# An attention block with its gradients on one core: a product moved to per-head pieces, a re-ordered iteration, reserved VectorE slots, and V transposed as float32 pairs

## Chip, cores, metric

The kernel runs on one core of a Trainium2 chip. The metric is the device time of one execution in microseconds, median of several runs. "Granted clock" is the share of the full TensorE (PE) clock that the throttle let through.

## The reference

A decode step (two batches, one query each) of an attention block and a ReLU MLP, with all gradients (shortened):

```python
def _A_ref(x, k_cache, v_cache, wq, wo):      # x: 2x1x640, caches: 2x32x4096x128, bf16
    q = (x @ wq).reshape(B, Sq, Hq, Dh).transpose(0, 2, 1, 3)
    scores = jnp.einsum("bhqd,bhkd->bhqk", q, k_cache) * (Dh ** -0.5)
    p = _softmax(scores, axis=-1)
    o = jnp.einsum("bhqk,bhkd->bhqd", p, v_cache)
    return o.transpose(0, 2, 1, 3).reshape(B, Sq, Hq * Dh) @ wo
h  = x + _A_ref(_layernorm(x), k_cache, v_cache, wq, wo)
h2 = h + relu(_layernorm(h) @ w1) @ w2
# outputs: h2 and the gradients of x, both caches, wq, wo, w1 and w2
```

Each cache holds 64 MiB and both have gradients as large. V is read twice, so the kernel moves 372.7 MB.

## The kernel before

Pass 1 is a software pipeline over 64 (batch, head) pairs: iteration `i` transposes K of pair `i` on PE and multiplies it by q, makes the softmax of pair `i-1`, and finishes the value product of pair `i-2`. `yield` marks the places where background work (`bg`) may be put in. The code issues the instructions in this order; the timeline of the changed kernel below shows VectorE at its own in that order (226.65 to 227.89 us).

```python
def p1_iter(i, dve_group):
    # step 0: c["KT0"] = transpose_group(c["K"], 0)       PE transposes, ScalarE copies to SBUF
    # step 1: u_half(0), KT1, max over partitions (PE) and gmax (VectorE), m_part(0)
    # step 2: scores group 0, KT2, exp (ScalarE), u_half(1), m_part(1)
    # step 3: scores group 1, KT3, m_part(2), pk_part(0)  pk = K times softmax, VectorE
    # step 4: scores group 2, m_part(3), pk_part(1)
    # step 5: m_part(4), m_part(5), sum and its reciprocal, P_bf, pk_part(2)   (VectorE)
    # step 6: scores group 3, rmax, m_part(6), pk_part(3)
    ...
    # step 7
        m_part(7)
        nc.scalar.activation(out=MT[:], in_=r["m"][:, 0:128], func=ACT.Copy, scale=r["rtot"][:, 0:1])
        nc.scalar.activation(out=OU[:, br, hr, :], in_=r["m"][:, 128:130], ...)   # attention output of a head
```

After the last head of a batch a background generator does that batch's middle, beginning with the product with `wo`:

```python
def middle_gen(b):
    nc.vector.tensor_copy(out=OFc[:, :, b], in_=OU[:, b, :, 0])
    yield
    a_ps = pst([128, ND], FP32, "mid", "a_ps")
    for c in range(ND):
        for h in range(H):
            nc.tensor.matmul(a_ps[:, c:c + 1], lhsT=wo_t[:, h, c * 128:(c + 1) * 128], rhs=OFc[:, h, b:b + 1],
                             start=(h == 0), stop=(h == H - 1))
            if h % (4 if b == 0 else 8) == 3:
                yield
    ...  # norm, MLP, its gradients, reductions on VectorE (ttr), gradient of the attention output
```

Pass 2 reads V again (`W`), transposes it for the product with that gradient, and writes two outer products per pair, the gradients of V and of K. It starts 15 iterations after the last head of batch 0; until pass 1 ends, every second iteration carries one step of it ("the mix").

## Time and profile before

| | before |
|---|---|
| time, median | 1045.99 us |
| DMA busy (16 engines' mean) | 954 of 1044 us, 391 GB/s while busy |
| PE / VectorE / ScalarE busy | 81% / 67% / 62% |
| mean granted clock | 0.74 |

The prediction below shows the stages, chain and waits. One line is added here. It is the share of each engine in the chain of work that ended last, followed back from the last instruction, from the page:

```profile
PE 40%; DMA 26%; DVE 16%; issue 10%; ACT 5%; POOL 1%; SPq 0%; POOLq 0%; ACTq 0%; DVEq 0%
```

And these are two cost groups of the page: line, engine, operation, output<-inputs, shapes, count, busy us and mean ns, idle time before it and what ended it. They are the transposes of V and ScalarE's copies of all transposes.

```profile
L279 ACT COPY t_sb<-t_ps 128x1024 bf16<-128x1024 bf16 x489 | 490.4, 1013 | 190.4 <-PE t_ps L274 184.1
L274 PE MATMUL t_ps<-ident_bf,Wt 128*128 128x128 bf16 x2048 | 239.2, 289 | 16.6 <-DMA Wt<-in_A_v_cache_dram 15.3
```

A transpose of V kept PE busy for 239.2/2048 = 117 ns.

### The profile page before, as it was taken

How to read it: one execution, taken by the hardware profiler on the slowest of the kernel's cores; microseconds unless marked ns; L12 is line 12 of the kernel's file. 1: busy time of each engine (PE TensorE's matmuls, PEld its weight loads, DVE VectorE, ACT ScalarE, POOL GpSimd, SP SyncE). 2: the span in 40 equal slices, each digit the busy share in tenths (PEclk: the TensorE clock that was granted, in tenths of full speed). 3: DMA queues.
4: the chain of work that ended last, by engine and by line, in shares of the span. 5: the costliest groups of instructions: out<-in, count | busy, mean ns of one | idle time of the engine just before them, and what ended most of it. 6: DMA issues, size and time to landing. Idle time of an engine off the chain costs nothing.

```text
span 1044.0 us, 32292 instructions
## 1 busy us (share of the span) xinstructions
PE 843.8 (81%) x14111; PEld 730.7 (70%) x14111; DVE 698.8 (67%) x1654; ACT 644.8 (62%) x985; POOL 95.2 (9%) x216
## 2 busy tenths in 40 slices
PE   6999989999998988878895665547998987676795
PEld 5988888889987887778784554436675765665553
DVE  3656777766549777776665768777876755566465
ACT  4555555467766586667674564546777766555684
POOL 0000000000000000000011111111111111111121
PEclk9988999899969889887875575566555555667555
DMA  9999999999857578898999999999899998999697
GB/s 350 382 400 405 363 364 379 347 349 351 323 206 282 205 278 314 346 379 342 363 413 425 371 384 394 355 402 361 326 412 422 398 393 329 421 422 401 231 374 319
DMA packets 59758, 372.70 MB, mean 357 GB/s; under 512 B 5760, under 2 KB 15424, under 8 KB 17376
## 3 DMA queue, kind: packets, MB, share of 16 engines
q1 hardware_dynamic: 38960, 221.50, 56.2%
q0 software_dynamic: 20656, 149.14, 34.7%
q8 instruction: 110, 1.80, 0.7%
q14 instruction: 32, 0.26, 0.1%
HBM read 221.48 MB, written 149.13 MB: 355 GB/s over the span
## 4 chain that ended last, share of the span: by engine, by line
PE 40%; DMA 26%; DVE 16%; issue 10%; ACT 5%; POOL 1%; SPq 0%; POOLq 0%; ACTq 0%; DVEq 0%
PE t_ps L274 16%; DMA out_dram<-gV 15%; PE m_ps L304 9%; DMA Wt<-in_A_v_cache_dram 6%; DVE pk L310 5%; DVE gK L550 4%; PE o_ps L652 4%; PE m_ps L320 4%; PE s_ps L285 3%; DVE junk L436 3%; ACT t_sb L279 2%; DMA Vt<-in_A_v_cache_dram 2%; DMA Kt<-in_A_k_cache_dram 2%; PE dp_ps L285 1%; DVE gV L550 1%
## 5 line engine op out<-in xcount | busy, mean ns | idle before, releaser
L279 ACT COPY t_sb<-t_ps 128x1024 bf16<-128x1024 bf16 x489 | 490.4, 1013 | 190.4 <-PE t_ps L274 184.1
L274 PE MATMUL t_ps<-ident_bf,Wt 128*128 128x128 bf16 x2048 | 239.2, 289 | 16.6 <-DMA Wt<-in_A_v_cache_dram 15.3
L274 PEld LDWEIGHTS <-Wt 128*128 128x128 bf16 x2048 | 185.4, 132 | 67.7 <-issue 50.0
L285 PEld LDWEIGHTS <-t_sb 128*128 128x128 bf16 x4096 | 171.1, 104 | 67.4 <-ACT t_sb L279 58.5
L310 DVE TENSOR_TENSOR pk<-Kt,ep 128x1024 bf16<-128x1024 bf16 x256 | 174.5, 683 | 45.0 <-ACT ep L353 41.2
L550 DVE TENSOR_TENSOR gV<-rb,pp 128x2048 bf16<-128x2048 bf16 x128 | 155.8, 1217 | 66.8 <-DMA out_dram<-gK 31.7
L550 DVE TENSOR_TENSOR gK<-rb,gsp 128x2048 bf16<-128x2048 bf16 x128 | 153.6, 1218 | 59.5 <-DMA out_dram<-gV 59.5
L304 PE MATMUL m_ps<-pk,Vt 128*128 128x129 bf16 x2048 | 193.3, 234 | 0.0
L274 PE MATMUL t_ps<-ident_bf,Kt 128*128 128x128 bf16 x2048 | 172.9, 234 | 2.3 <-DMA Kt<-in_A_k_cache_dram 2.3
L304 PEld LDWEIGHTS <-Vt 128*128 128x128 bf16 x2048 | 135.8, 104 | 4.5
L274 PEld LDWEIGHTS <-Kt 128*128 128x128 bf16 x2048 | 132.4, 104 | 3.6 <-DMA Kt<-in_A_k_cache_dram 2.7
L285 PE MATMUL dp_ps<-goc,t_sb 128*128 128x1 bf16 x2048 | 97.6, 169 | 45.7 <-ACT t_sb L279 43.4
L594 POOL DMA_DIRECT2D out_dram<-gV x64 | 34.2, 534 | 667.7 <-DVE gV L550 638.1
L285 PE MATMUL s_ps<-qc,t_sb 128*128 128x1 bf16 x2048 | 89.3, 164 | 4.2 <-DVE gsp L585 2.0
L406 ACT ACTIVATE MT<-m_ps,rtot 128x128 bf16<-128x128 f32 x64 | 23.5, 368 | 105.3 <-PE m_ps L304 105.3
L320 PEld LDWEIGHTS <-Kt 128*128 128x128 bf16 x2048 | 64.7, 97 | 20.3 <-issue 18.9
L277 DVE COPY t_sb<-t_ps 128x1024 bf16<-128x1024 bf16 x43 | 29.7, 690 | 71.6 <-PE t_ps L274 71.5
L320 PE MATMUL m_ps<-ep,Kt 128*128 128x1 bf16 x2048 | 70.8, 164 | 7.6 <-ACT OU L407 6.3
L655 ACT CAST ot<-o_ps 128x512 bf16<-128x512 f32 (+3 forms) x120 | 59.8, 526 | 11.7 <-PE o_ps L652 10.4
L564 ACT CAST rb<-rb_ps 128x256 bf16<-128x256 f32 x64 | 24.4, 381 | 49.7 <-DVE gK L550 37.9
L610 POOL DMA_DIRECT2D out_dram<-gK x64 | 34.0, 531 | 226.8 <-DVE gK L550 183.7
L436 DVE CUSTOM_DVE_ANT_0 junk<-wo_t,hbc 128x640 bf16<-128x640 bf16 x64 | 52.1, 815 | 0.1
(168 smaller groups left out, 703.2 us busy)
## 6 DMA issues: line engine op xcount, KB each, us to landing
Kt<-in_A_k_cache_dram SPq DMA_DIRECT2D x64, 1024.0 KB, 8.0
Vt<-in_A_v_cache_dram SPq DMA_DIRECT2D x64, 1024.0 KB, 7.6
Wt<-in_A_v_cache_dram SPq DMA_DIRECT2D x64, 1024.0 KB, 10.6
out_dram<-gV POOLq DMA_DIRECT2D x64, 1024.0 KB, 8.2
out_dram<-gK POOLq DMA_DIRECT2D x64, 1024.0 KB, 9.3
wo_t<-in_A_wo_dram SPq DMA_DIRECT2D x4, 1280.0 KB, 9.5
wqs<-in_A_wq_dram SPq DMA_DIRECT2D x5, 1024.0 KB, 17.4
out_dram<-ot POOLq DMA_DIRECT2D x5, 1024.0 KB, 5.5
```

The source lines that it names most:

```text
L274: nc.tensor.transpose(t_ps[:, j, :], nat[:, g * GT + j, :], ident_bf[:])
L279: nc.scalar.copy(out=t_sb[:], in_=t_ps[:])
L285: nc.tensor.matmul(dst[:, sc:sc + 1], lhsT=t_sb[:, j, :], rhs=vec, start=True, stop=True)
L304: nc.tensor.matmul(r["m"][:, 0:129], lhsT=r["V"][:, sc, :], rhs=r["pk"][sc // GT][:, sc % GT, 0:129], start=False, stop=(sc == NSC - 1))
L310: nc.vector.tensor_tensor(out=pk[:, :, 0:128].rearrange("p s (a two) -> p s a two", two=2), in0=p["K"][:, sl, :].rearrange("p s (a two) -> ...
L320: nc.tensor.matmul(r["m"][:, 129:130], lhsT=r["K"][:, sc, :], rhs=r["ep"][:, sc, 0:1], start=(sc == 0), stop=False)
L436: nc.vector.tensor_tensor_reduce(out=junk[0:kc, 0:width], in0=in0, in1=in1, scale=1.0, scalar=0.0, op0=ALU.mult, op1=ALU.add, accum_out=acc)
L550: nc.vector.tensor_tensor(out=pairs_view(dst[:, sl, :]), in0=row.rearrange("p (a two) -> p a two", two=2)[:, None, :, :].to_broadcast([128 ...
L594: nc.gpsimd.dma_start(out=natural(out_3, b, h), in_=gV[:])
L610: nc.gpsimd.dma_start(out=natural(out_2, bp, hp), in_=gK[:])
L652: nc.tensor.matmul(o_ps[0:P, 0:nn], lhsT=L[:, bass.ds(c0 + k, P, step=cc)], rhs=R[:, n0:n0 + nn], start=True, stop=True)
L655: nc.scalar.copy(out=ot[0:P, k, n0:n0 + nn], in_=o_ps[0:P, 0:nn])
```

## The change

Its intent: spread the wo product over pass 1 so that pass 2 starts after 12 iterations rather than 15; give PE work while the softmax chain goes over VectorE; put the 0.8 us reductions into chosen gaps; and halve ScalarE's copies of V by moving pairs of bf16 as one float32. The core of the diff, cut:

```diff
+    def a_head():                       # wo product per head
+        b, h = pairs[a_next[0]]
+        if h == 0:
+            a_bank[0] = pst([128, ND], FP32, "a", "a_ps")
+        nc.vector.tensor_copy(out=OFc[:, h, b:b + 1], in_=OU[:, b, h, 0:1])
+        for c in range(ND):
+            nc.tensor.matmul(a_bank[0][:, c:c + 1], lhsT=wo_t[:, h, c * 128:(c + 1) * 128], rhs=OFc[:, h, b:b + 1],
+                             start=(h == 0 and c == 0), stop=(h == H - 1 and c == ND - 1))
+        a_next[0] += 1
...
+            if k == 5:                  # after step 5 of the iteration
+                a_heads(i)              # up to two a_head()s, from iteration 15 on
...                                      # iteration re-ordered
             c["KT0"] = transpose_group(c["K"], 0)
+            c["KT1"] = transpose_group(c["K"], 1)
...
+    def turn():                         # VectorE slots: a reduction waits for its turn
+        while slot[0] <= 0:
+            yield 0.0
+        slot[0] -= 1
...                                      # V as float32 pairs
+        natf = nat[:].bitcast(FP32)
+        for j in range(GT // 2):
+            cc = (g * GT) // 2 + j
+            nc.tensor.transpose(t_ps[:, j, :], natf[:, 2 * cc:2 * cc + 2, :].rearrange("p c k -> p (c k)"), ident_f[:])
...
-    M0_ITERS = 15
+    M0_ITERS = 12
...                                      # V of pass 2 asked for one step ahead
+        ahead = plan[n + 1][1] if n + 1 < len(plan) and ii is not None else jj
```

The row of coefficients for the pairs (`gom`) is made by a small selection product, `pair_rows`. The order of pass 2 also changed (gradient of K first), the final outer products got a third PSUM bank, and small softmax results moved into the bank of the scores. Smaller edits are not shown: the weights load in another order, and the credit by which background work is put in has a cap.

More of the change, by code (lines that the diff above doesn't have):

```diff
@@ L54 @@
     GH = 8
-    NMT = 52
+    NMT = 48
     def f_kc(c):
@@ L69 @@
     ps = ctx.enter_context(tc.tile_pool(name="ps", bufs=1, space=bass.MemoryType.PSUM))
-    PSB = {"tps": 2, "sps": 3, "m": 1, "tiny": 1, "mid": 1}
+    PSB = {"tps": 2, "sps": 3, "m": 1, "a": 1, "mid": 1}
     def pst(shape, dtype, tag, name):
@@ L90 @@
                             fill=1.0, base=0, pattern=[[-1, 128]], channel_multiplier=1)
-    ones_bf = const.tile([128, 128], BF16)
-    nc.vector.memset(ones_bf[:], 1.0)
-    ones_f32 = const.tile([128, 128], FP32)
-    nc.vector.memset(ones_f32[:], 1.0)
+    ident_f = const.tile([128, 128], FP32)
+    nc.vector.tensor_copy(out=ident_f[:], in_=ident_bf[:])
+    sel = const.tile([128, 2, 2, 64], BF16)
+    nc.gpsimd.memset(sel[:], 0.0)
+    for par in range(2):
+        nc.gpsimd.affine_select(out=sel[:, par, :, :], in_=sel[:, par, :, :], compare_op=ALU.not_equal,
+                                fill=1.0, base=-par, pattern=[[0, 2], [-2, 64]], channel_multiplier=1)
+    ones_bfc = const.tile([128, 1], BF16)
+    nc.vector.memset(ones_bfc[:], 1.0)
+    ones_bf = ones_bfc[:].to_broadcast([128, 128])
+    ones_f32c = const.tile([128, 1], FP32)
+    nc.vector.memset(ones_f32c[:], 1.0)
+    ones_f32 = ones_f32c[:].to_broadcast([128, 128])
     xr = cols.tile([4 * ND, 128], BF16)
@@ L112 @@
     goc = cols.tile([128, H, B], BF16)
+    gom = cols.tile([128, H, B, 2, 2], BF16)
+    nc.gpsimd.memset(gom[:], 0.0)
     negdot = cols.tile([128, H, B], FP32)
@@ L127, in colsum @@
         t = pst([128, 16], FP32, "mid", "csum")
-        nc.tensor.matmul(t[:, 0:n], lhsT=ones_f32[:], rhs=src, start=True, stop=True)
+        nc.tensor.matmul(t[:, 0:n], lhsT=ones_f32, rhs=src, start=True, stop=True)
         return t
@@ L226, with pair_rows @@
     wo_r = A_wo.rearrange("(c p) d -> p c d", p=128)
+    def pair_rows(dst, src, hs, bs):
+        n, nb = hs.stop - hs.start, bs.stop - bs.start
+        t = pst([128, 2, n, nb], FP32, "mid", "pr_ps")
+        for par in range(2):
+            nc.tensor.matmul(t[:, par, :, :], lhsT=sel[:, par, :, :].rearrange("p c k -> p (c k)"),
+                             rhs=src[:, hs, bs], start=True, stop=True)
+        for c in range(2):
+            rows = slice(64 * c, 64 * c + 64)
+            for par in range(2):
+                nc.vector.tensor_copy(out=dst[rows, hs, bs, par, c], in_=t[rows, par, :, :])
     def load_weights(k):
@@ L285, in matvec_group, with pair_transpose, pair_matvec @@
             nc.tensor.matmul(dst[:, sc:sc + 1], lhsT=t_sb[:, j, :], rhs=vec, start=True, stop=True)
+    def pair_transpose(nat, g, dve=False):
+        t_ps = pst([128, GT // 2, 128], FP32, "tps", "t_ps")
+        natf = nat[:].bitcast(FP32)
+        for j in range(GT // 2):
+            cc = (g * GT) // 2 + j
+            nc.tensor.transpose(t_ps[:, j, :], natf[:, 2 * cc:2 * cc + 2, :].rearrange("p c k -> p (c k)"), ident_f[:])
+        t_sb = mats.tile([128, GT // 2, 128], FP32, tag="XT", bufs=5, name="t_sb")
+        if dve:
+            nc.vector.tensor_copy(out=t_sb[:], in_=t_ps[:])
+        else:
+            nc.scalar.copy(out=t_sb[:], in_=t_ps[:])
+        return t_sb
+    def pair_matvec(dst, t_sb, g, vecs):
+        v = t_sb[:].bitcast(BF16).rearrange("p j (k two) -> p j k two", two=2)
+        for j in range(GT // 2):
+            sc = g * GT + 2 * j
+            for par in range(2):
+                nc.tensor.matmul(dst[:, sc:sc + 2], lhsT=v[:, j, :, par], rhs=vecs[:, par, :],
+                                 start=(par == 0), stop=(par == 1))
     def natural(cache, b, h):
@@ L330, in p1_iter @@
             u_half(0)
-        if c is not None:
-            c["KT1"] = transpose_group(c["K"], 1)
+            u_half(1)
+            give(r["Kg"])
         if p is not None:
@@ L335, in p1_iter @@
             bhp = bp * H + hp
-            mx_ps = pst([1, 128], FP32, "tiny", "mx_ps")
-            nc.tensor.matmul(mx_ps[:], lhsT=p["rmax"][:], rhs=ident_bf[:], start=True, stop=True)
+            mx = p["bank"][0:1, 64:192]
+            nc.tensor.matmul(mx, lhsT=p["rmax"][:], rhs=ident_bf[:], start=True, stop=True)
             gmax = small.tile([1, 1], BF16, tag="gmax", name="gmax")
-            nc.vector.reduce_max(out=gmax[:], in_=mx_ps[:], axis=AX.X)
+            nc.vector.reduce_max(out=gmax[:], in_=mx, axis=AX.X)
         if r is not None:
@@ L343, in p1_iter @@
         if c is not None:
-            c["s"] = pst([128, NSC], FP32, "sps", "s_ps")
+            c["bank"] = pst([128, 512], FP32, "sps", "s_ps")
+            c["s"] = c["bank"][:, 0:NSC]
             matvec_group(c["s"], c.pop("KT0"), 0, q)
             c["KT2"] = transpose_group(c["K"], 2)
+        if r is not None:
+            m_part(1)
+        yield
+        if c is not None:
+            matvec_group(c["s"], c.pop("KT1"), 1, q)
         if p is not None:
-            nb_ps = pst([128, 1], FP32, "tiny", "nb_ps")
-            nc.tensor.matmul(nb_ps[:], lhsT=ones_bf[0:1, :], rhs=gmax[:], start=True, stop=True)
+            nbp = p["bank"][:, 200:201]
+            nc.tensor.matmul(nbp, lhsT=ones_bf[0:1, :], rhs=gmax[:], start=True, stop=True)
             nb = small.tile([128, 1], FP32, tag="nb", name="nb")
-            nc.scalar.mul(out=nb[:], in_=nb_ps[:], mul=-SCALE)
+            nc.scalar.mul(out=nb[:], in_=nbp, mul=-SCALE)
             ep = small.tile([128, NSC, 2], BF16, tag="ep", name="ep")
@@ L356, in p1_iter @@
         if r is not None:
-            u_half(1)
-            give(r["Kg"])
-            m_part(1)
+            m_part(2)
+        if c is not None:
+            c["KT3"] = transpose_group(c["K"], 3, dve_group)
         yield
-        if c is not None:
-            matvec_group(c["s"], c.pop("KT1"), 1, q)
-            c["KT3"] = transpose_group(c["K"], 3, dve_group)
-        if r is not None:
-            m_part(2)
         if p is not None:
             pk_part(0)
-        yield
+            pk_part(1)
+        if r is not None:
+            m_part(3)
         if c is not None:
@@ L371, in p1_iter @@
         if r is not None:
-            m_part(3)
+            m_part(4)
         if p is not None:
-            tot_ps = pst([128, NSC], FP32, "tiny", "tot_ps")
-            nc.tensor.matmul(tot_ps[:], lhsT=ones_bf[:], rhs=ep[:, :, 0], start=True, stop=True)
-            pk_part(1)
+            totp = p["bank"][:, 256:256 + NSC]
+            nc.tensor.matmul(totp, lhsT=ones_bf, rhs=ep[:, :, 0], start=True, stop=True)
         yield
         if r is not None:
-            m_part(4)
             m_part(5)
+        if c is not None:
+            matvec_group(c["s"], c.pop("KT3"), 3, q)
+            rmax = small.tile([128, 1], BF16, tag="rmax", name="rmax")
+            nc.vector.reduce_max(out=rmax[:], in_=c["s"], axis=AX.X)
+            c["rmax"] = rmax
         if p is not None:
+            pk_part(2)
             tot = small.tile([128, 1], FP32, tag="tot", name="tot")
-            nc.vector.reduce_sum(out=tot[:], in_=tot_ps[:], axis=AX.X)
+            nc.vector.reduce_sum(out=tot[:], in_=totp, axis=AX.X)
             rtot = small.tile([128, 1], FP32, tag="rtot", name="rtot")
@@ L388, in p1_iter @@
             p["rtot"] = rtot
-            pk_part(2)
         yield
-        if c is not None:
-            matvec_group(c["s"], c.pop("KT3"), 3, q)
-            rmax = small.tile([128, 1], BF16, tag="rmax", name="rmax")
-            nc.vector.reduce_max(out=rmax[:], in_=c["s"][:], axis=AX.X)
-            c["rmax"] = rmax
         if r is not None:
@@ L410, in p1_iter, with a_heads @@
         yield
+    a_next = [0]
+    a_bank = [None]
+    def a_head():
[7 more added lines that the diff above has]
+        a_next[0] += 1
+    def a_heads(i):
+        for _ in range(2):
+            g = a_next[0]
+            if g > i - 3 or g >= NP1:
+                return
+            b, h = pairs[g]
+            if b == 0 and i < W_AT[1 + h * 4 // H] + 4 or b > 0 and ("a", b - 1) not in done:
+                return
+            a_head()
     def bcast_cols(colsrc, n, kc_of, dst):
@@ L437, in ttr @@
                                        op0=ALU.mult, op1=ALU.add, accum_out=acc)
+    slot = [99]
+    def turn():
+        while slot[0] <= 0:
+            yield 0.0
+        slot[0] -= 1
     def one(src, b):
@@ L446, in go_group @@
         for k in range(GH):
+            yield from turn()
             ttr(wo_t[:, g * GH + k, :], hbc[:], go32[:, k:k + 1], D)
@@ L449, in go_group @@
         nc.vector.tensor_copy(out=goc[:, hs, b], in_=go32[:])
+        yield
+        pair_rows(gom, goc, hs, slice(b, b + 1))
         pr = small.tile([128, GH], FP32, tag="pr", bufs=1, name="pr")
@@ L454, in go_group @@
         d_ps = pst([128, 2, GH], FP32, "mid", "d_ps")
-        nc.tensor.matmul(d_ps[:, 0, :], lhsT=ones_f32[:], rhs=pr[:], start=True, stop=True)
+        nc.tensor.matmul(d_ps[:, 0, :], lhsT=ones_f32, rhs=pr[:], start=True, stop=True)
         for k in range(GH):
@@ L467, in middle_gen @@
     def middle_gen(b):
-        nc.vector.tensor_copy(out=OFc[:, :, b], in_=OU[:, b, :, 0])
-        yield
-        a_ps = pst([128, ND], FP32, "mid", "a_ps")
-        for c in range(ND):
-            for h in range(H):
-                nc.tensor.matmul(a_ps[:, c:c + 1], lhsT=wo_t[:, h, c * 128:(c + 1) * 128], rhs=OFc[:, h, b:b + 1],
-                                 start=(h == 0), stop=(h == H - 1))
-                if h % (4 if b == 0 else 8) == 3:
-                    yield
+        while a_next[0] < (b + 1) * H:
+            a_head()
+            yield
+        a_ps = a_bank[0]
         at_bf = small.tile([128, ND], BF16, tag="at_bf", bufs=1, name="at_bf")
@@ L481, in middle_gen @@
         nc.vector.tensor_copy(out=h32[:, 0, :], in_=h1c[:, :, b])
-        yield
+        yield ("a", b)
         yield from ln_fwd(h32[:], 1, x2c[:, :, b:b + 1], rstd2[:, b:b + 1])
@@ L507, in middle_gen @@
             for k in range(3):
+                yield from turn()
                 ttr(w1_t[:, c, k * FW:(k + 1) * FW], fbc[:, k * FW:(k + 1) * FW], gx2p[:, c, k:k + 1], FW)
@@ L540, in ga_gen @@
                 kc = f_kc(c)
+                yield from turn()
                 ttr(w2_t[0:kc, c, :], gbc[0:kc, :], ga[0:kc, b, c:c + 1], D, kc)
@@ L553, in outer_half @@
             in1=colp[:, sl, None, :].to_broadcast([128, HALF, 64, 2]), op=ALU.mult)
-    def p2_rows(j):
-        b, h = pairs[j]
-        rb_ps = pst([128, 256], FP32, "tiny", "rb_ps")
-        nc.tensor.matmul(rb_ps[:, 0:128], lhsT=goc[:, h, b:b + 1].to_broadcast([128, 128]), rhs=ident_bf[:],
-                         start=True, stop=True)
-        nc.tensor.matmul(rb_ps[:, 128:256], lhsT=qsc[:, h, b:b + 1].to_broadcast([128, 128]), rhs=ident_bf[:],
-                         start=True, stop=True)
-        rb = mats.tile([128, 256], BF16, tag="rb", bufs=3, name="rb")
-        nc.scalar.copy(out=rb[:], in_=rb_ps[:])
-        pp = small.tile([128, NSC, 2], BF16, tag="pp", name="pp")
-        nc.gpsimd.tensor_copy(out=pp[:], in_=P_bf[:, b * H + h, :, None].to_broadcast([128, NSC, 2]))
-        S2.setdefault(j, {}).update(rb=rb, pp=pp)
     def p2_iter(j):
@@ L572, in p2_iter @@
         p = S2[j - 1] if j - 1 in S2 else None
-        if c is not None:
-            b, h = pairs[j]
-            go = goc[:, h, b:b + 1]
-            if "rb" not in c:
-                p2_rows(j)
-            c["T0"] = transpose_group(c["W"], 0)
-            gV = take("g", [128, NSC, 128], "gV")
-            outer_half(gV, c["rb"][:, 0:128], c["pp"], 0)
         if p is not None:
             bp, hp = pairs[j - 1]
-            matvec_group(p["dp"], p.pop("T3"), 3, goc[:, hp, bp:bp + 1])
+            pair_matvec(p["dp"], p.pop("T3"), 3, gom[:, hp, bp, :, :])
             gsp = small.tile([128, NSC, 2], BF16, tag="gsp", name="gsp")
@@ L587, in p2_iter @@
                 in1=P_bf[:, bp * H + hp, :, None].to_broadcast([128, NSC, 2]), op0=ALU.add, op1=ALU.mult)
-        yield
         if c is not None:
-            c["dp"] = pst([128, NSC], FP32, "sps", "dp_ps")
-            c["T1"] = transpose_group(c["W"], 1)
-            matvec_group(c["dp"], c.pop("T0"), 0, go)
-            outer_half(gV, c["rb"][:, 0:128], c["pp"], 1)
-            nc.gpsimd.dma_start(out=natural(out_3, b, h), in_=gV[:])
-            give("g")
-        yield
-        if c is not None:
-            c["T2"] = transpose_group(c["W"], 2)
-            matvec_group(c["dp"], c.pop("T1"), 1, go)
+            b, h = pairs[j]
+            go = gom[:, h, b, :, :]
+            bank = pst([128, 512], FP32, "sps", "dp_ps")
+            for k, col in enumerate((goc, qsc)):
+                nc.tensor.matmul(bank[:, 128 + k * 128:256 + k * 128],
+                                 lhsT=col[:, h, b:b + 1].to_broadcast([128, 128]), rhs=ident_bf[:],
+                                 start=True, stop=True)
+            c["dp"] = bank[:, 0:NSC]
+            rb = mats.tile([128, 256], BF16, tag="rb", bufs=3, name="rb")
+            nc.scalar.copy(out=rb[:], in_=bank[:, 128:384])
+            pp = small.tile([128, NSC, 2], BF16, tag="pp", name="pp")
+            nc.gpsimd.tensor_copy(out=pp[:], in_=P_bf[:, b * H + h, :, None].to_broadcast([128, NSC, 2]))
+            c.update(rb=rb, pp=pp)
+            c["T0"] = pair_transpose(c["W"], 0)
         if p is not None:
@@ L603, in p2_iter @@
         yield
-        if c is not None:
-            c["T3"] = transpose_group(c["W"], 3)
-            give(c["Wg"])
-            matvec_group(c["dp"], c.pop("T2"), 2, go)
         if p is not None:
@@ L613, in p2_iter @@
         yield
-        if j + 1 < NP1 and ("go", (j + 1) // H, ((j + 1) % H) // GH) in done:
-            p2_rows(j + 1)
+        if c is None:
+            return
+        c["T1"] = pair_transpose(c["W"], 1)
+        pair_matvec(c["dp"], c.pop("T0"), 0, go)
+        yield
+        c["T2"] = pair_transpose(c["W"], 2)
+        pair_matvec(c["dp"], c.pop("T1"), 1, go)
+        yield
+        c["T3"] = pair_transpose(c["W"], 3)
+        give(c["Wg"])
+        pair_matvec(c["dp"], c.pop("T2"), 2, go)
+        gV = take("g", [128, NSC, 128], "gV")
+        outer_half(gV, c["rb"][:, 0:128], c["pp"], 0)
+        yield
+        outer_half(gV, c["rb"][:, 0:128], c["pp"], 1)
+        nc.gpsimd.dma_start(out=natural(out_3, b, h), in_=gV[:])
+        give("g")
         yield
@@ L650, in outer_rows @@
                     fw[0] += 1
-                    o_ps = pst([128, 512], FP32, "mid" if fw[0] % 2 else "m", "o_ps")
+                    o_ps = pst([128, 512], FP32, ("mid", "m", "a")[fw[0] % 3], "o_ps")
                     nc.tensor.matmul(o_ps[0:P, 0:nn], lhsT=L[:, bass.ds(c0 + k, P, step=cc)], rhs=R[:, n0:n0 + nn],
@@ L733, in bg_step @@
         q = (bg, bg2)[k]
-        credit[k] = credit[k] + rate if q else 0.0
+        credit[k] = min(credit[k] + rate, 2.0) if q else 0.0
         while q and credit[k] > 0.0:
-            credit[k] -= bg_one(q)
+            took = bg_one(q)
+            credit[k] -= took
+            if took == 0.0:
+                break
     def bg_until(mark):
+        slot[0] = 99
         while mark not in done:
             assert bg_one(bg) > 0.0, mark
-    M0_ITERS = 15
+    M0_ITERS = 12
     P2_AT = H + 2 + M0_ITERS
@@ L764 @@
                 queue.append(("K", ii))
-        if jj is not None and jj < NP1:
-            queue.append(("W", jj))
+        ahead = plan[n + 1][1] if n + 1 < len(plan) and ii is not None else jj
+        if ahead is not None and ahead < NP1 and ("W", ahead) not in queue:
+            queue.append(("W", ahead))
         if ii is not None and 1 <= ii <= NP1:
@@ L769 @@
         if ii in W_AT:
-            queue.append(("w", (5, 4, 0, 1, 2, 3)[W_AT.index(ii)]))
+            queue.append(("w", (5, 0, 1, 2, 3, 4)[W_AT.index(ii)]))
     queue.insert(0, ("wq", 0))
@@ L793, with p2_step @@
     fin = None
-    for n, (i, j) in enumerate(plan):
-        gens = []
-        if i is not None:
-            if i % QP == 0 and 1 <= i // QP < NQ:
-                q_piece(i // QP)
-                pump()
-            gens.append(p1_iter(i, i < H + 1))
+    g2 = None
+    MIXED = {1: 2, 3: 1, 4: 1, 6: 1}
+    REST = {1: 1}
+    def p2_step():
+        nonlocal g2
+        try:
+            next(g2)
+        except StopIteration:
+            g2 = None
+    for n, (i, j) in enumerate(plan):
+        if i is not None and i % QP == 0 and 1 <= i // QP < NQ:
+            q_piece(i // QP)
+            pump()
         if n + 3 < len(plan) and plan[n + 3][1] is not None:
@@ L803 @@
         if j is not None:
+            while g2 is not None:
+                p2_step()
             if j < NP1:
                 bg_until(("go", j // H, (j % H) // GH))
-            gens.append(p2_iter(j))
+            g2 = p2_iter(j)
         if i is None and j >= H - 1:
@@ L814 @@
             bg.append(("ga", ga_gen()))
-        rate = RATES[0 if i is not None and i <= H + 1 else 1 if j is None else 2 if i is not None else
-                     3 if j <= H else 4]
-        while gens:
-            for g in list(gens):
-                try:
-                    next(g)
-                except StopIteration:
-                    gens.remove(g)
-                    continue
+        rate = RATES[0 if i is not None and i <= H + 1 else 1 if j is None and i < P2_AT else
+                     2 if i is not None else 3 if j <= H else 4]
+        if i is None:
+            slot[0] = 99
+            while g2 is not None:
+                p2_step()
                 pump()
@@ L826 @@
                 bg_step(1, RATE2)
+            continue
+        at = MIXED if j is not None else REST
+        for k, _ in enumerate(p1_iter(i, i < H + 1)):
+            for _ in range(at.get(k, 0)):
+                if g2 is not None:
+                    p2_step()
+            if k == 5:
+                a_heads(i)
+            pump()
+            slot[0] = ((2 if rate == RATES[1] else 1) if k == 1 else 1 if k == 6 else 0) if i < P2_AT else int(k == 6)
+            bg_step(0, rate)
+            bg_step(1, RATE2)
         if i is not None and i in (H + 1, NP1 + 1):
```

## The prediction

> **What bounds the kernel now.** I read the page's first two sections, then the same span cut into five stages, then the chain that ended last, then the waits of the stages that looked thin. The kernel runs a first pass over 64 (batch, head) pairs (reads K and V, makes the softmax row and a 128x128 product), a background that turns each batch's result into the gradient of the attention output, and a second pass over the same pairs (reads V again, writes the gradients of V and K). The stages are: first pass alone while weights load (0 to 250 us), first pass with batch 0's middle computation (250 to 363), both passes mixed, two first-pass iterations to one second-pass step (363 to 525), second pass (525 to 965), tail. I took the borders from the count of row-max reductions, one per first-pass iteration: 34, 14 and 16 of them in the first three stages. Columns: stage, busy us of PE, PEld, DVE, ACT, POOL, then granted clock, DMA share, GB/s.
>
> ```profile
> 0.00:250.00 250.00, 223.76 (x4582) 206.24 (x4582) 164.60 (x556) 138.44 (x243) 1.87 (x8) 0.95 0.97 371
> 250.00:363.00 113.00, 104.71 (x2200) 97.27 (x2197) 76.28 (x276) 75.70 (x125) 0.00 (x0) 0.89 0.75 267
> 363.00:525.00 162.00, 136.84 (x2630) 127.14 (x2627) 116.14 (x313) 109.18 (x168) 10.52 (x23) 0.86 0.86 333
> 525.00:965.00 440.00, 317.48 (x4172) 260.61 (x4168) 298.71 (x461) 271.16 (x378) 70.46 (x158) 0.58 0.97 390
> 965.00:1044.00 79.00, 61.00 (x546) 39.48 (x546) 43.05 (x49) 50.35 (x75) 12.34 (x28) 0.50 0.76 307
> ```
>
> The DMA column decides. It is full (0.97) at the start and in the second pass; it is thin in the middle computation (0.75), the mix (0.86) and the tail (0.76). Idle DMA time is length times one minus share: 7.5 + 28 + 23 + 13 + 19 = about 90 us. The other 954 us move 372.7 MB, 391 GB/s. So **the program is DMA-bound with 90 us of holes**, and only holes can be won unless bytes per busy microsecond change. The chain agrees: in the second pass it alternates between stores and the outer products that wait for a store's buffer.
>
> ```profile
> 598.01 11.35 DMA out_dram<-gV
> 609.39 2.37 DVE gK L550 x2
> 612.82 3.27 issue
> 616.10 9.83 DMA out_dram<-gV
> ```
>
> In the middle stage PE is busy for 93%, but an iteration takes 113/14 = 8.1 us there, against (247.0 - 222.6)/4 = 6.1 us just before it (starts of the row-max reductions), without that background. Part is added work, part waiting, and the clock fell to 0.73 in 287 to 325 us. The waits of 287 to 365 us show the VectorE pieces of the middle computation (some 0.8 us each) and ScalarE's copies breaking the softmax chain:
>
> ```profile
> DVE pk L310 <- ACT ep L353: 8.2, 6, 2.4
> DVE gmax L339 <- PE mx_ps L337: 5.7, 4, 2.4
> PE nb_ps L349 <- DVE gmax L339: 3.5, 4, 1.3
> ```
>
> In the mix, PE waits for V to arrive, about 2.5 us in most of the second-pass steps, and for a PSUM tile shared by the softmax and the row broadcasts:
>
> ```profile
> PE t_ps L274 <- DMA Wt<-in_A_v_cache_dram: 15.3, 6, 3.2
> PE rb_ps L559 <- DVE tot L383: 4.7, 8, 1.4
> ```
>
> [...]a 128x128 f32 load of the d_ps group has a median of 240 ns, the bf16 loads a mean of 97 to 132. [...]The trace: 1013 ns for 1024 bf16 elements and 595 ns for 512 f32, 0.82 ns per element.[...]
>
> **The change, part by part.**
>
> *V as f32 pairs.* Per second-pass step, 32 bf16 transposes become 16 of f32, and four ScalarE copies of 1024 bf16 become four of 512 f32. ScalarE: 4 x (1013 - 595) = 1.7 us saved per step, 64 steps, 107 us of busy time. The product with the output gradient stays 32 loads and 32 matmuls, with a stride of two elements in the weights and two columns instead of one; I take it as unchanged (eight took 0.34 us). PE: a bf16 group of eight takes 0.61 us at full clock (timeline at 440 us), 2.4 us per step. Four f32 transposes limited by their load, with 0.15 us per load (two f32 loads of d_ps took 0.30 us together), are 0.6 us; at one matmul's pace, 0.3 us. So PE gains 0 to 1.2 us per step. In the second pass almost none of this is on the path: DMA share is 0.97. I give 2 of its 13 idle us back.
>
> *First pass reordered.* It has the same matmuls, copies and VectorE work. K's second transpose group and both halves of the u product come early, so PE has work while the max goes through VectorE and ScalarE. In the first stage PE is 90% busy and DMA 97%: gain about 0.5 us.
>
> *VectorE slots and wo product per head.* The wo product of batch 0 was 160 matmuls in 40 background turns, five iterations of eight turns, all after head 31. Now five matmuls follow each head while the first pass runs, so the middle gets shorter and the second pass may start after 12 iterations, not 15. The 0.8 us reductions go only into chosen gaps, at most three per iteration. The reductions needed before the first second-pass step, 15 + 8 = 23, fill eight of those twelve iterations; norms and broadcasts take the rest, so 12 is tight. I expect 12 iterations at 6.5 us = 78 us with a DMA share near 0.9: 8 us idle instead of 28.
>
> *The mix* becomes ten pairs of iterations instead of nine. One pair moves four loads of the first pass and one load and two stores of the second, 7 x 1.049 = 7.34 MB. At 333/0.86 = 387 GB/s per busy time that is 19.0 us. A pair took 2 x 162/16 = 20.3 us; PE's work in it was 17.1 us and falls if anything. Loading V one step ahead and moving the shared PSUM tile into the score bank remove the two waits above. So the mix goes to its DMA floor: 190 us with 4% idle, 8 us instead of 23.
>
> *Tail.* The final outer products get a third PSUM bank, and each step's ScalarE copies shrink by 1.7 us. I take 6 of 19 us.
>
> Idle sum after: 7 + 8 + 8 + 11 + 13 = 47 us. The saving is 90 - 47 = 43 us: 1046 - 43 = **1003 us**.
>
> **The rivals.**
>
> [...]
>
> *The wait moves.* The twelve iterations do not suffice, and the kernel must force the middle's remainder before the first second-pass step; or the second pass's new order waits for the three store buffers in VectorE's queue, with the first pass behind it. For it: [...]outer products already waited 45 us for stores in 525 to 700. Then the mix stays at 20 us per pair and half the gain is lost: about 1025 us. I give it 20%.
>
> *Transfers are better, not only denser.* A thinner ScalarE and PE could also end the slow stretches inside the second pass; with all its holes and half the tail gone the time is about 985 us. Against: its share is already 0.97, and what slows single packets is not visible in these views.
>
> **Range and chances.** Two per cent is 21 us, so faster means below 1025 us; 43 us expected leaves twice that. The middle case has most of the weight, the waiting rival sits at the border[...]. Range 972 to 1030 us; faster 0.84, same 0.09, slower 0.07.
>
> **What will show it.** Right: f32 transposes at no more than twice a bf16 one each, V copies near 0.6 us, the first gradient store some 40 us earlier (its outer product now stands at 385 us in the chain), iterations near 6.5 us in the middle stage, the mix at about 19 us per pair with DMA share over 0.93, total idle DMA near 47 us at 391 GB/s per busy time. Wrong: PE over 90% busy in the second pass[...], a burst of reductions just before the first second-pass step (12 too few), VectorE waits on stores in the mix, or a changed rate per busy microsecond, which I assume constant and cannot derive.

The sum keeps all its terms: 47 us idle, 43 us saved, 1003 us. PE's part of the float32 transposes was the author's estimate: 0.6 us for a group of four from two f32 loads in 0.30 us (d_ps), or 0.3 us as half of the 0.61 us of eight bf16 transposes. A whole rival is cut: that the float32 transposes are slow enough to make PE the bound, near 1080 us, at 7%. It made up the slower side of the chances, and is what "PE over 90% busy in the second pass" was to show.

## The result

| | before | changed |
|---|---|---|
| time, median | 1045.99 us | 1157.45 us |
| DMA busy | 954 of 1044 us | 960 of 1163 us |
| PE / VectorE / ScalarE busy | 81% / 67% / 62% | 77% / 61% / 46% |
| mean granted clock of the profiled run | 0.74 | 0.68 |

The ratio is 1.106, 95% interval 1.100 to 1.112: slower by over 10%. A ratio here is the mean time of one kernel's fast runs over that of the other's fast runs of the same rounds, so it is not quite the ratio of the medians. DMA does the same work in about the same busy time, at 372.6 MB/960 us = 388 GB/s. The loss is idle DMA: 203 us instead of 90.

The changed kernel by stage, columns as in the prediction (PE, PEld, DVE, ACT, POOL, granted clock, DMA share, GB/s):

```profile
0.00:125.00 125.00, 107.13 (x2198) 101.67 (x2199) 76.17 (x266) 66.63 (x116) 2.93 (x12) 0.92 1.00 390
125.00:335.00 210.00, 168.32 (x2950) 162.97 (x2949) 106.74 (x386) 86.17 (x154) 0.00 (x0) 0.72 0.64 237
335.00:460.00 125.00, 104.47 (x1719) 99.63 (x1719) 66.63 (x230) 59.97 (x103) 0.94 (x2) 0.69 0.52 187
460.00:640.00 180.00, 145.75 (x2568) 139.21 (x2565) 114.51 (x317) 94.16 (x165) 10.48 (x24) 0.77 0.86 326
640.00:1070.00 430.00, 323.12 (x3117) 249.84 (x3116) 292.66 (x494) 204.08 (x393) 74.17 (x146) 0.56 0.92 365
```

The first 125 us are as good as before (DMA share 1.00). Then the DMA share falls to 0.64 with the clock at 0.72. The starts of the row-max reductions, one per iteration, say when: up to the one of iteration 15 they stand 6 to 9 us apart, and after it mostly 9 to 12 us. Iteration 15 is the first one with a per-head wo product, which comes after its row max. One interval, from 155.7 to 161.7 us, is back at 6.0 us, and it is one in which no wo matmul starts. Iterations 16 to 33 average 10.20 us, against 6.77 us before. The last reduction of pass 1 stands at 634 us instead of 520 us, which is nearly all of the loss.

The waits of 126 to 334 us (who waited for whom, total us, times, longest):

```profile
PEld L474 <- issue: 41.1, 19, 2.5
PE a_ps L474 <- DVE OFc L471: 39.8, 19, 2.4
DVE t_sb L302 <- PE t_ps L299: 39.0, 16, 3.5
```

PE stands 2.1 us (39.8 us in 19 waits) in front of the wo matmuls and waits for a copy of 128 numbers. The timeline of one iteration shows what the copy itself waits for (start, length, engine, line; in brackets the engine's idle time before it and what ended it):

```profile
226.65 0.69 DVE L358 TENSOR_TENSOR pk<-Kt,ep 128x1024 bf16<-128x1024 bf16 x1
227.25 0.18 DVE L362 COPY pk<-ep 128x8 bf16<-128x8 bf16 x1
227.32 0.19 DVE L440 TENSOR_REDUCE tot<-s_ps 128x1 f32<-128x32 f32 x1
227.54 0.16 DVE L442 RECIPROCAL rtot<-tot 128x1 f32<-128x1 f32 x1
227.74 0.24 DVE L443 TENSOR_SCALAR P_bf<-ep,rtot 128x32 bf16<-128x32 bf16 x1
227.89 0.21 DVE L471 CAST OFc<-OU 128x1 bf16<-128x1 f32 x2
...
228.09 0.39 PE L474 MATMUL a_ps<-OFc,wo_t 128*128 128x1 bf16 x10 [2.01 <-DVE OFc L471]
...
231.63 0.28 DVE L389 TENSOR_REDUCE gmax<-s_ps 1x1 bf16<-1x128 f32 x1 [2.11 <-PE s_ps L387]
...
235.38 0.69 DVE L302 COPY t_sb<-t_ps 128x1024 bf16<-128x1024 bf16 x1 [3.47 <-PE t_ps L299]
```

The head's output had been ready since the iteration before. But the copy is issued after this iteration's products, sum, reciprocal and probabilities, and VectorE takes them in that order: 1.24 us pass from the start of the product at 226.65 us to that of the copy at 227.89 us. While PE stands, VectorE catches up; then VectorE idles (2.11 and 3.47 us) until PE has made what it needs. The two engines take turns where they overlapped before: in 125 to 335 us PE is busy for 168.3 us and VectorE for 106.7 us, against 194.2 and 147.0 us in the kernel before. Chain and cost groups of the changed kernel:

```profile
PE 52%; DVE 20%; DMA 17%; issue 6%; ACT 4%; POOL 0%; SPq 0%; DVEq 0%; POOLq 0%; ACTq 0%
```

```profile
L319 PE MATMUL t_ps<-ident_f,Wt 128*128 128x128 f32 x1024 | 236.6, 382 | 0.0
L324 ACT COPY t_sb<-t_ps 128x512 f32<-128x512 f32 x256 | 148.6, 588 | 172.0 <-PE t_ps L319 166.6
```

DMA's share of the chain fell from 26% to 17% and PE's rose from 40% to 52%. This shift is not the mark of the loss, though: e1_copy_early below, which is as fast as the kernel before, has PE at 52% and DMA at 18%. Half as many transposes of V cost as much PE time as before: 236.6/1024 = 231 ns each, against 117 ns.

### The profile page after: what moved, and what is told of

It reads as the page before. It is cut to its first block, busy times and chain, and to the rows that moved or that the text cites. A ratio compares the mean times of both kernels' runs of the same rounds, so it can differ in the third digit from the quotient of the medians.

```text
span 1162.7 us, 30385 instructions
## 1 busy us (share of the span) xinstructions
PE 896.5 (77%) x13103; PEld 793.8 (68%) x13103; DVE 714.8 (61%) x1749; ACT 540.5 (46%) x985; POOL 107.2 (9%) x220
## 4 chain that ended last, share of the span: by engine, by line
PE 52%; DVE 20%; DMA 17%; issue 6%; ACT 4%; POOL 0%; SPq 0%; DVEq 0%; POOLq 0%; ACTq 0%
PE t_ps L299 14%; PE m_ps L352 10%; PE t_ps L319 8%; DVE pk L358 6%; DMA out_dram<-gK 5%; DMA Kt<-in_A_k_cache_dram 5%; DMA out_dram<-gV 4%; PE o_ps L730 4%; PE m_ps L368 4%; DVE gV L635 4%; DVE gK L635 3%; PE s_ps L310 3%; PE dp_ps L332 2%; DVE junk L513 2%; DMA out_dram<-ot 2%
## 5 line engine op out<-in xcount | busy, mean ns | idle before, releaser
L304 ACT COPY t_sb<-t_ps 128x1024 bf16<-128x1024 bf16 x233 | 230.0, 1015 | 113.8 <-PE t_ps L299 113.3
L319 PE MATMUL t_ps<-ident_f,Wt 128*128 128x128 f32 x1024 | 236.6, 382 | 0.0
L324 ACT COPY t_sb<-t_ps 128x512 f32<-128x512 f32 x256 | 148.6, 588 | 172.0 <-PE t_ps L319 166.6
L352 PE MATMUL m_ps<-pk,Vt 128*128 128x129 bf16 x2048 | 226.9, 252 | 0.7 <-issue 0.7
L299 PE MATMUL t_ps<-ident_bf,Kt 128*128 128x128 bf16 x2048 | 203.8, 268 | 8.4 <-DMA Kt<-in_A_k_cache_dram 5.5
L319 PEld LDWEIGHTS t_ps<-ident_f,Wt 128*128 128x128 f32 x1024 | 166.2, 198 | 23.1 <-PE o_ps L730 14.5
L299 PEld LDWEIGHTS <-Kt 128*128 128x128 bf16 x2048 | 170.4, 123 | 10.7 <-DMA Kt<-in_A_k_cache_dram 6.3
L352 PEld LDWEIGHTS <-Vt 128*128 128x128 bf16 x2048 | 152.3, 111 | 8.6 <-issue 1.8
L332 PE MATMUL dp_ps<-gom,t_sb 128*128 128x2 bf16 x2048 | 96.6, 168 | 34.4 <-ACT t_sb L324 33.7
L389 DVE TENSOR_REDUCE gmax<-s_ps 1x1 bf16<-1x128 f32 x64 | 17.9, 280 | 116.5 <-PE s_ps L387 116.5
L733 ACT CAST ot<-o_ps 128x512 bf16<-128x512 f32 (+3 forms) x120 | 57.5, 523 | 15.9 <-PE o_ps L730 10.2
```

Source lines behind the costliest of these rows:

```text
L299: nc.tensor.transpose(t_ps[:, j, :], nat[:, g * GT + j, :], ident_bf[:])
L304: nc.scalar.copy(out=t_sb[:], in_=t_ps[:])
L319: nc.tensor.transpose(t_ps[:, j, :], natf[:, 2 * cc:2 * cc + 2, :].rearrange("p c k -> p (c k)"), ident_f[:])
L324: nc.scalar.copy(out=t_sb[:], in_=t_ps[:])
L332: nc.tensor.matmul(dst[:, sc:sc + 2], lhsT=v[:, j, :, par], rhs=vecs[:, par, :], start=(par == 0), stop=(par == 1))
L352: nc.tensor.matmul(r["m"][:, 0:129], lhsT=r["V"][:, sc, :], rhs=r["pk"][sc // GT][:, sc % GT, 0:129], start=False, stop=(sc == NSC - 1))
```

## The experiments

The theory (S) after the first look: the per-head copy makes PE wait for VectorE's queue, and the stall also throttles PE's clock (0.72 in 125 to 335 us, 0.93 before). Rivals: the re-ordered iteration, the slots or the float32 transposes cost the time. Thirteen kernels ran, in four sets; kernels of a set share the runs of the kernel before. All gave correct results. The idle matmuls of two of them wrote only to unused PSUM columns.

| run | edit | median us | before in its set | ratio (95%) |
|---|---|---|---|---|
| e1_copy_early | copy early | 1047.8 | 1050.7 | 0.998 (0.995 to 1.000) |
| e2_wo_at_end | wo product in one piece again | 1044.6 | 1050.7 | 0.995 (0.992 to 0.997) |
| e3_bf16_v | V as bf16 again | 1156.2 | 1050.7 | 1.100 (1.098 to 1.103) |
| e4_fill | idle matmuls, which waited themselves | 1143.3 | 1050.7 | 1.088 (1.086 to 1.090) |
| e5_late_rows | e1 + row selection later | 1046.3 | 1048.4 | 0.997 (0.994 to 1.001) |
| e6_no_w_ahead | e1 + V not asked for ahead | 1032.6 | 1048.4 | 0.984 (0.979 to 0.989) |
| e7_no_slots | e1 + no slots | 1041.0 | 1048.4 | 0.992 (0.988 to 0.996) |
| e8_bf16_v | e1 + V as bf16 | 1046.3 | 1048.4 | 0.999 (0.995 to 1.004) |
| e9_wo_alone | before + wo product per head | 1143.3 | 1047.5 | 1.091 (1.088 to 1.094) |
| e10_wo_early | e9 with the copy early | 1052.9 | 1047.5 | 1.006 (1.003 to 1.009) |
| e11_both | e6 and e7 together | 1029.0 | 1047.5 | 0.983 (0.978 to 0.988) |
| e12_p2_order | e6 + old order of pass 2 | 1035.5 | 1047.5 | 0.989 (0.985 to 0.992) |
| e13_fill_free | idle matmuls in the stall | 1106.1 | 1048.3 | 1.057 (1.052 to 1.062) |

### The copy: e1, e2, e9, e10

```diff
# e1_copy_early, on the changed kernel
+    def a_copy():
+        b, h = pairs[a_copied[0]]
+        nc.vector.tensor_copy(out=OFc[:, h, b:b + 1], in_=OU[:, b, h, 0:1])
+        a_copied[0] += 1
     def a_head():
-        nc.vector.tensor_copy(out=OFc[:, h, b:b + 1], in_=OU[:, b, h, 0:1])
+        if a_copied[0] == a_next[0]:
+            a_copy()
...
+            if k == 1:                                   # early in the iteration
+                while a_copied[0] <= min(i - 3, NP1 - 1):
+                    a_copy()
             if k == 5:
                 a_heads(i)
```

> Changed kernel, one edit: the small VectorE copy of each head's attention output is issued early in the iteration, the five wo matmuls stay where they were. Theory S (PE stands about 2 us per iteration because that copy is behind the reductions and products in VectorE's order, and the stall throttles the PE clock): from iteration 15 on iterations fall from about 10.5 to 6.5 us, total 990 to 1030 us, granted clock in 125 to 335 us over 0.9. Rival R (the re-ordered iteration, the slots or the f32 transposes are to blame): total stays at 1140 us or more.

Measured 1047.8 us. Moving one small copy took back all of the 110 us (ratio 0.998 to the kernel before, against 1.106), though not the 990 to 1030 us that I had expected. Iterations 16 to 33 are back at 6.79 us. In the stage of 125 to 335 us clock and DMA share recover:

```profile
125.00:335.00 210.00, 191.64 (x4181) 182.91 (x4178) 154.54 (x555) 126.28 (x224) 0.00 (x0) 0.93 0.85 321
```

In its timeline the copy comes right behind the maximum, and the wo matmuls of that head start later without any wait:

```profile
206.19 0.14 DVE L471 CAST OFc<-OU 128x1 bf16<-128x1 f32 x1
...
209.49 0.26 PE L482 MATMUL a_ps<-OFc,wo_t 128*128 128x1 bf16 x5
```

```diff
# e2_wo_at_end, on the changed kernel: middle_gen as before (a yield per 8 heads), and
-            if k == 5:
-                a_heads(i)
```

> Changed kernel with the wo product put back into one piece after the last head of a batch (20 background turns, still 12 iterations, so a part of the middle is forced out before the first second-pass step). Theory S: the iterations 15 to 33 are back at 6 to 7 us, total 1010 to 1070 us. Rival R: 1140 us or more.

Measured 1044.6 us, as expected. Twelve iterations are then too few: iteration 46 follows 23.5 us after iteration 45. Seven of the 0.8 us reductions stand in a row there, from 332.1 to 338.1 us: the rest of the middle is forced out.

```diff
# e9_wo_alone, on the kernel BEFORE (small softmax results in the score bank, to free a PSUM bank)
+            if k == 6 and i is not None:       # ahead of step 6, that is after step 5
+                a_heads(i)                     # copy and matmuls together
# e10_wo_early adds
+            if k == 2 and i is not None:       # after step 1
+                while a_copied[0] <= min(i - 3, NP1 - 1):
+                    a_copy()
```

> The kernel before with one part of the change alone: the wo product per head, copy and matmuls together in the iteration, at the same place (the small softmax results move into the score bank to free a PSUM bank; iteration order, bf16 V and 15 iterations as before). Theory L (copy and matmuls close a loop between PE and VectorE, in whatever order the iteration has): slower than before by 60 to 130 us, 1105 to 1180 us. Rival (it needs the new iteration order): within 2% of before.

> The same as e9_wo_alone with the copy issued early. Theory L: the loss is gone, 1030 to 1055 us. Otherwise 1105 us or more.

Measured 1143.3 and 1052.9 us. This one part makes the old kernel 9.1% slower, in its old iteration order and with bf16 V; with the copy early the loss is gone but for 0.6%. So the new order is not needed for the harm. The waits of e9_wo_alone in 150 to 340 us have the same signature:

```profile
PE a_ps L424 <- DVE OFc L421: 38.0, 17, 3.9
DVE gmax L339 <- PE s_ps L337: 34.3, 17, 3.2
DVE t_sb L277 <- PE t_ps L274: 31.3, 13, 3.5
```

### Wait or clock: e4, e13

PE stood 2.1 us per iteration, but iterations grew by 3.4 us (10.20 less 6.79). In iterations 16 to 33 the trace's clock records have PE at half clock for 96 of 173 us, against 7 of 115 us before. PE's 16 waits for the copy in these iterations are 1.8 to 2.4 us long. Filling the stall with useless matmuls was to keep PE active without removing the wait.

```diff
# e4_fill, on the changed kernel
             if k == 5:
+                for _ in range(24):
+                    nc.tensor.matmul(S1[i - 1]["bank"][:, 300:428], lhsT=ident_bf[:], rhs=ident_bf[:], ...)
                 a_heads(i)
# e13_fill_free: the same into the unused columns 128:256 of the wo product's own bank, start=False
```

> Changed kernel plus 24 idle 128x128 matmuls into an unused piece of a PSUM bank, just ahead of the wo matmuls in iterations 15 to 64: the wait of PE is filled, not removed. If half of the lost 4 us per iteration is the throttled clock: iterations fall to about 8 us, total 1030 to 1100 us. If the lost time is the wait alone and the clock does not matter: total 1150 to 1200 us. Rival R: 1150 to 1220 us.

Measured 1143.3 us, between the two expectations, and the trace showed why the run tells little: the filler itself waited for VectorE's read of the sum in the same tile (30.2 us in 18 waits from 150 to 340 us) and ran after the wait. It lengthened what it should have filled, so I repeated it in a bank that only PE touches.

> The changed kernel with 24 idle matmuls ahead of the wo matmuls as in e4_fill, but into the bank of the wo product, which only PE touches, so that they run while PE waits and not after a wait of their own. If the throttled clock makes up about half of the lost 4 us per iteration: granted clock near 0.9 in 125 to 335 us, iterations of 8 to 9 us, total 1070 to 1110 us. If the wait loop alone sets the iteration: 10 us or more, total 1140 us or more.

Measured 1106.1 us, 51 us faster than the changed kernel with 1,152 more matmuls in it. Stage and waits of e13_fill_free, to be set beside those of the changed kernel:

```profile
125.00:335.00 210.00, 188.18 (x3999) 180.27 (x3998) 126.66 (x452) 103.79 (x185) 0.00 (x0) 0.95 0.75 276
```

```profile
PE a_ps L474 <- DVE OFc L471: 17.7, 21, 1.6
```

The clock is at 0.95 instead of 0.72, and iterations 16 to 33 take 8.60 us. PE still waits 0.8 us behind the filler (17.7 us in 21 waits), so the filler did not delay the wo matmuls. Taken this way, 1.6 of the 3.4 us lost per iteration go with the slowed clock, and 1.8 us remain with the loop between PE and VectorE. Of the 110 us between the changed kernel and e1_copy_early these are about 51 and 58 us; the three kernels ran in different sets, whose medians of the kernel before differ by up to 5 us.

### The float32 pairs: e3, e8

```diff
# e3 on the changed kernel, e8 on e1: for all groups
-        c["T1"] = pair_transpose(c["W"], 1)
-        pair_matvec(c["dp"], c.pop("T0"), 0, go)
+        c["T1"] = transpose_group(c["W"], 1)
+        matvec_group(c["dp"], c.pop("T0"), 0, go)
...                                     # and no pair_rows
```

> Changed kernel with the second pass's V transposed as bf16 again, and without the row selection that the pairs need. Theory S: first pass unchanged, the time after the first pass shorter by up to 15 us because PE no longer waits behind the row selection; total 1140 to 1165 us. Rival F (the f32 transposes are the cause): total near 1050 us.

> e1_copy_early with V as bf16 again and without the row selection. If the f32 pairs are worth the ScalarE time they save once the stall is gone: 1055 to 1075 us. If that saving is off the path: 1040 to 1050 us.

Measured 1156.2 and 1046.3 us. In these two settings the pairs are worth nothing measurable: e8 is at 0.999 of before, and e1 at 0.998. They neither caused the loss nor gained anything there; without them the kernel of e6 below was not run.

### Where the forecast gain went: e5, e6, e7, e11, e12

After e1 the kernel still had 90 us of idle DMA, where I had forecast 47. All of these start from e1_copy_early.

```diff
# e5_late_rows
         yield
-        pair_rows(gom, goc, hs, slice(b, b + 1))
         pr = small.tile([128, GH], FP32, tag="pr", bufs=1, name="pr")
...
         yield
         yield
+        pair_rows(gom, goc, hs, slice(b, b + 1))
# e6_no_w_ahead
-        ahead = plan[n + 1][1] if n + 1 < len(plan) and ii is not None else jj
+        ahead = jj
# e7_no_slots: turn() returns at once.   e11_both: e6 and e7.
```

> e1_copy_early plus one edit: the row selection for the pairs is issued two background turns later, so that PE does not reach it while VectorE is still in outer products. Theory W (where the rest of the forecast gain went: new PE waits in the second pass, 29 us of them on goc in 560 to 930 us): 1025 to 1040 us. Rival B (loads wait for buffers, DMA is the bound there): no change, 1043 to 1050 us.

> e1_copy_early with the second pass's V queued in its own step again, not one step ahead. Theory B (the V loaded ahead keeps one of seven load buffers longer and delays the K loads of the first pass, on which PE then waits): 1025 to 1042 us, and no waits on K in the mix but waits on V as before. Rival: V then comes late, 1048 to 1065 us.

> e1_copy_early without the VectorE slots (the reductions go wherever a background turn comes). If the slots help as meant: 1052 to 1075 us. If they only hold the middle back: 1030 to 1045 us.

> The changed kernel with the copy early, V not queued ahead and no slots: if the gains of e6 and e7 add, 1018 to 1030 us; if they are the same gain, 1030 to 1040 us.

e5 changed nothing (1046.3 us), but it did not remove the wait that it was made for. From 560 to 930 us PE waited 21.6 us at the row selection and 7.8 us right after it, together as long as the 29.1 us of e1, so e5 tests nothing. e8 does: it has no row selection, PE waits 7.1 us at that place, and the time is the same. e6 gave 1032.6 us. In the mix of e1_copy_early (335 to 520 us) PE waited for K while a V of pass 2 held a load buffer early:

```profile
PEld L299 <- DMA Kt<-in_A_k_cache_dram: 21.0, 6, 5.5
PE t_ps L299 <- DMA Kt<-in_A_k_cache_dram: 20.0, 6, 5.3
```

In e6 PE waits 2.7 us for K and 6.0 us for V in the mix, and a pair of iterations takes (506 - 347)/17 x 2 = 18.7 us, where e1 needed 20.6 us. e7, without slots, is at 1041.0 us (ratio 0.992 against 0.998, intervals that just overlap): in sum the slots did not help. By stage they did two opposite things. Without them an iteration of the middle stage takes 8.5 us instead of 7.95, but a pair of the mix takes 19.0 us instead of 20.6, although PE waits for K as long as in e1 (19.1 us). e11 combines both edits, 1029.0 us at 0.983. That lies at the edge of the range expected for added gains, but is no more than e6 alone within the intervals; it is 1.7% faster than the kernel before. Its pairs of the mix take 17.6 us, its iterations of the middle 8.8 us. The stages of e6_no_w_ahead, the last idle time to place:

```profile
240.00:335.00 95.00, 86.32 (x1712) 82.22 (x1710) 65.80 (x250) 59.86 (x101) 0.00 (x0) 0.83 0.68 247
335.00:520.00 185.00, 165.66 (x3157) 157.90 (x3154) 137.45 (x380) 113.68 (x204) 12.69 (x29) 0.86 0.94 366
520.00:965.00 445.00, 323.86 (x3167) 249.18 (x3168) 294.16 (x483) 210.44 (x404) 75.54 (x150) 0.58 0.93 367
```

Its idle DMA is 0.32 x 95 = 30 us in the middle stage, 11 us in the mix, 31 us in pass 2, some 10 us at both ends: 82 us. Pass 2 alone misleads here: with the tail it idles 38 us, where the kernel before idled 13 + 19 = 32 us. Most of the idle time that pass 2 gained had stood in the tail. For pass 2 I tried the old order.

```diff
# e12_p2_order, on e6: gradient of V in the first two quarters of a step, gradient of K in the last two,
# row broadcasts one step ahead when pass 2 runs alone; float32 pairs kept
```

> e6_no_w_ahead with the second pass in the order of the kernel before (V gradient first, row broadcasts made a step ahead), f32 pairs kept. If the new order of the second pass costs the 20 us of DMA idle that it shows over the kernel before: 1010 to 1022 us. If not: 1028 to 1040 us.

Measured 1035.5 us, no gain over e6. Its DMA share in pass 2 is 0.94, and that of e8, without row selection, is 0.94 too, for 0.93 in e1 and e6. So neither the order nor the row selection accounts for more than a small part of the idle time of pass 2, and the rest stays open. So does the middle stage. In e6 it holds three slow spots of 11 to 13 us per iteration (iterations 35 and 36, 42, 45 and 46), and PE waits of 3.1 and 1.7 us on the norm's sums lie in the same stretch, but no run takes these apart.

## Why the prediction was wrong

- **The step that failed is "five matmuls follow each head while the first pass runs, so the middle gets shorter".** I counted these matmuls as moved at no cost. They need a VectorE copy, and it stands in VectorE's order behind the softmax work of the same iteration. What the runs showed in its place: PE waited 2.1 us for that copy, and iterations of pass 1 took 10.2 us instead of 6.8. The cost was 110 us (e1 against the changed kernel; e9 shows it in the kernel before).
- **The rival "the wait moves" had the right kind of trouble in the wrong place.** I looked for it in pass 2 and at the twelfth iteration, gave it 20% and 1025 us. It came in pass 1, in nearly every iteration from the fifteenth on.
- **The clock was not in the sum.** I had read 0.73 in 287 to 325 us as a symptom and worked with constant durations. e13 gives it 1.6 of the 3.4 us per iteration.
- **First pass reordered, 0.5 us: too low for the stage.** Iterations 16 to 33 take 6.79 us in e1 and 6.77 us before, but those of e1 carry the wo product; in e2, without it, they take 6.52 us. Before iteration 34 DMA idles 0.01 x 240 = 2 us in e6 for 7.5 us before. The new order, the slots and the order of the weights' loads were not taken apart.
- **Float32 pairs: ScalarE's part was right, 588 ns for 595 forecast, and off the path.** PE's part, 0 to 1.2 us saved per step, was at the lower end: eight bf16 transposes took 0.61 us at full clock, and so did four float32 ones (medians of all groups in the traces). So the rival that is cut, PE as the bound, did not happen: in 640 to 1070 us of the changed kernel PE is busy for 323 of 430 us.
- **Middle stage, 6.5 us per iteration: mis-sized.** It measured 7.95 us in e1 and (333.9 - 235.8)/12 = 8.2 us in e6 (iterations 34 to 45), no less than the (363.2 - 247.0)/15 = 7.75 us before; 30 us idle for 8 forecast. Only the three iterations fewer were won. e2 shows that twelve iterations are too few without the per-head product.
- **Mix, 19.0 us per pair: about right once one of two edits was undone.** It was 20.6 us in e1, 19.0 in e7, 18.7 in e6 and 17.6 in e11, so it was no floor: in that stretch e11 moved 7.03 MB per pair for 7.34 counted, at 401 GB/s per busy time for 387. Asking for V one step ahead, which I had counted as a gain, cost about 15 us (e1 to e6); PE's waits for K in the mix went from 20.0 to 2.7 us. That these waits alone set the length of the mix is not shown, since e7 shortened it with the waits in place.
- **Tail and pass 2 were mis-sized in opposite directions.** In e6 the tail idles 0.10 x 68 = 7 us (13 forecast) and pass 2 31 us (11 forecast), together 38 us for 24.
- **Right:** bytes per busy microsecond stayed nearly the same, 388 to 392 GB/s in the changed kernel, e1 and e6, so idle DMA was the right quantity for the loss of 110 us. For the small gain of e6 it was half of the matter: summed from the packets of the profiled runs, its idle time is 5 us less than before and its busy time 6 us less.
- **Misread: the first gradient store, forecast some 40 us earlier.** Once the stall is gone it comes 20 us earlier, at 350.1 us in e1 for 369.7 us before. The outer product at 385 us, from which I counted, belongs to the second step; the first one starts at 366.9 us and is not in the chain.

## What to carry to other kernels

When work is spread into a pipelined loop, ask for each new instruction what stands ahead of it on its producer's engine, not only whether its data are ready. Here a copy of 0.15 us at the wrong place turned two overlapping engines into two that took turns, 10.20 us per iteration instead of 6.79 (e1). Issue such producers early and consumers late, and look at the clock too: here it was 0.72 in 125 to 335 us with PE's stall and 0.95 with the stall filled (e13). Look also at what a prefetch from a shared pool takes from other loads: with V asked for one step ahead PE waited 20.0 us for K in the mix, without it 2.7 us (e1, e6). And before a wait is blamed or cleared by an experiment, check in its trace that the wait is gone (e5).
